# Forgetting attention and a bilinear FFN on one core: the decay moved from TensorE to a DVE pass, q and k loaded six tokens to a partition, scores and older values in one PE visit

## The chip, the cores and the metric

The kernel runs on one NeuronCore of a Trainium2 chip. The metric is device time in microseconds (us) of one execution, lower is better. The median of three runs of the kernel before is 453.05 us (452.42 to 453.66).

Engine names are those of the profile: PE is the matrix engine (PEld its weight loads), DVE the vector engine, ACT the scalar engine, POOL the GpSimd engine, and SP the engine that issues most DMAs. PSUM is the memory that matmuls write; it has eight banks of 512 float32 per partition, and all eight are in use.

## The reference

Eight batches of eight heads, 576 tokens, head dimension 64. Attention has a learned forgetting: each token has a gate f, and a score is lowered by the summed logarithms of the gates between the two tokens. Heads are joined to 512 columns per token and go through a bilinear FFN.

```python
q, k, v: (8, 8, 576, 64); f: (8, 8, 576); w_a, w_b: (512, 1536); w_out: (1536, 512)
scores = q @ k.T / sqrt(64)
cum    = cumsum(log(clip(f, 1e-4, 1)), axis=-1)
scores = where(causal, -1e9, scores + cum[..., :, None] - cum[..., None, :])
x      = softmax(scores) @ v            # heads joined: (4608, 512)
out    = ((x @ w_a) * (x @ w_b)) @ w_out
```

The row term `cum[..., :, None]` is the same for a whole row and falls out of the softmax, so that the kernel adds only the column term.

## The kernel before

**Pairs.** Two heads make a pair (four pairs in a batch, 32 in all, index t in the code). One head of a pair lies on partitions 0 to 63, the other on 64 to 127. The 576 rows of scores of a head are five blocks i of 128 (the last has 64). Causality leaves 128*(i+1) columns in block i.

**Scores (L457 to L494).** `qk_group` writes one of four groups of blocks, (1, 0), (2), (3), (4), into a PSUM tile `sc` of two banks (two such tiles). Three kinds of matmuls add up in it: q times k (`sc<-kT,qT`, and `sc<-kT,tT` for the last 64 rows, which have tiles of their own), a matrix of ones times the two float16 rows (high and low part) of the decay (`sc<-cr,ones`), and a mask of -60000 above the diagonal (`sc<-neg,low`). Each is issued twice, once for each half of the array's rows, and the two halves run side by side.

**Softmax.** `do_max` (L502) takes the negated row maximum of both heads with one DVE reduction from PSUM; `do_exp` (L527, L531) runs on ACT with the maximum as bias, reads PSUM, and sums as it goes, which makes a second instruction, ACTIVATION_READ_ACCUMULATOR; DVE takes reciprocals of the sums (L538, L540), POOL multiplies (L548). The probabilities PA and PB (float16) are transposed by DMA (L558), in batch 0 by PE (L564). `do_pv` (L588) and `do_pv4` (L601, the last 64 rows) multiply with v into one PSUM bank `pv`, and DVE copies to `xT` (L608, L612).

**FFN (L729 to L762).** `ffn(t0, n)` takes n tokens: 12 times a group of four matmuls for w_a (`psa`) and four for w_b (`psb`), an ACT copy of psa (L263), a DVE product (L743), then for each 128 tokens 12 matmuls with w_out (`pso`, L752), a copy and a store. Tokens are cut into 256, 256 and eight times 512. psa, psb, pso and the transposed tiles share three PSUM banks called `ff`.

**Inputs.** q, k, v come by DMAs from SP, 128 tokens to 128 partitions, so that a packet is the 256 bytes of one head's token. They are cast to float16 (L261 to L267; POOL from batch 1 on). q and k are transposed by PE in batches 0 and 1 (L300) and by DMA later. Weights come in 36 DMAs of 256 KB into a ring `wl` of four and are cast by DVE or POOL (L451).

**The order.** `schedule()` (L144 to L209) is a list scheduler inside the kernel. It knows a written duration for every operation, priorities, how many buffers each ring has, and the room in the DMA queue, and it places all operations in one order; each engine's queue holds its instructions in that order, and no engine overtakes. Attention has priorities by batch, and the FFN's matmuls (priority 5000 and over) fill what is left on PE. A change of PE's tile shape counts 0.1 us there.

Of the kernel before, what the change touches and what calls it, by code (L numbers as in the profile page):

```python
# [25 lines left out]
def kernel(  # L26
# [28 lines left out]
    HP = [slice(0, 64), slice(64, 128)]  # L55

# [4 lines left out]
    ones16 = perm.tile([128, 128], FP16, tag="ones16", name="ones16")  # L61
    cone = perm.tile([BH, S], FP16, tag="cone", name="cone")
# [3 lines left out]
    def constants():  # L66
        nc.gpsimd.memset(warm, 1.0)
        nc.gpsimd.memset(cone, 1.0)
        make_identity(nc, ident16)
        nc.gpsimd.memset(ones16, 0.0)  # L70
# [3 lines left out]
        for h in range(2):  # L74
            nc.gpsimd.memset(ones16[64 * h:64 * h + 2, :], 1.0)
            nc.gpsimd.affine_select(out=neg64[HP[h], :], in_=neg64[HP[h], :],
                                    compare_op=mybir.AluOpType.not_equal, fill=NEGBIG, base=0,
                                    pattern=[[-1, 64]], channel_multiplier=1)
            for half in range(2):
                x = low[half][HP[h], :]  # L80
                nc.gpsimd.affine_select(out=x, in_=x, compare_op=mybir.AluOpType.is_gt, fill=0.0,
                                        base=64 * half, pattern=[[-1, 128]], channel_multiplier=1)

    def paddings():
# [3 lines left out]
        nc.gpsimd.memset(crs[1], 0.0)  # L88
# [3 lines left out]
    wa16 = [perm.tile([128, DF], FP16, tag=f"wa16_{i}", name=f"wa16_{i}") for i in range(4)]  # L92
    wb16 = [perm.tile([128, DF], FP16, tag=f"wb16_{i}", name=f"wb16_{i}") for i in range(4)]
    wout16 = [perm.tile([128, DM], FP16, tag=f"wout16_{i}", name=f"wout16_{i}") for i in range(12)]
    nv = [perm.tile([128, NSB, H, D], FP16, tag=f"nv{i}", name=f"nv{i}") for i in range(2)]
    crs = [perm.tile([128, NP, S], FP16, tag=f"cr{i}", name=f"cr{i}") for i in range(2)]
    PB = [perm.tile([128, 13, 128], FP16, tag=f"PB{i}", name=f"PB{i}") for i in range(2)]

    RING = {"wl": 4, "n32": 4, "n16": 2, "n16t": 1, "nv": 2, "cr": 2, "qT": 2, "kT": 2, "tT": 2,
            "PA": 3, "PB": 2, "PTA": 3, "PTB": 2, "st": 6, "ht": 14, "a16": 3, "osb": 2,  # L100
            "sc": 2, "pv": 1, "ff": 3}
    wl_pool = pool("wl", RING["wl"])
    n32_pool = pool("n32", RING["n32"])
# [8 lines left out]
    dram = pool("scr", 1, space=bass.MemoryType.DRAM)  # L112
# [8 lines left out]
    PKT = {256: 0.021, 512: 0.031, 1024: 0.051, 2048: 0.095}  # L121

    class Op:


        def __init__(self, eng, dur, fn, deps=(), prio=0.0, land=None, mode=None, name="", bulk=False):
# [3 lines left out]
            self.bulk = bulk  # L130
# [12 lines left out]
    def schedule():  # L143
# [12 lines left out]
        def ready(o, e):  # L156
            t = 0.0
# [4 lines left out]
            for tag, _ in o.takes:  # L162
                lv = lives[tag]
                if len(lv) >= RING[tag]:
                    for u in lv[-RING[tag]]:
                        if u.done is None:
                            return None
                        t = max(t, u.done + SEM)
            return t

        while len(order) < len(ops):
            best = None
            for e, lst in pending.items():
                cand = None
                for o in lst:
# [3 lines left out]
                    at = max(r, free[e])  # L179
                    if o.bulk:  # L180
                        at = max(at, dma_free - BACKLOG)
                    if cand is None or at < cand[0] - 1e-9:
                        cand = (at, at + o.durs[e], o, e)
                        if at <= free[e] + 1e-9:
                            break
                if cand and (best is None or cand[0] < best[0] - 1e-9
# [6 lines left out]
            if e == "PE":  # L193
                if mode is not None and o.mode != mode:
                    at += 0.1
                mode = o.mode
            o.start = at
            free[e] = at + dur
# [18 lines left out]
    cum_d = dram.tile([2, BH, S], FP16, tag="cum_d", name="cum_d")  # L217
    cw = {}

    def f_load(_):  # L220
        for n in ("f", "l", "c"):
            cw[n] = wl_pool.tile([128, 576], FP32, tag="wl", name=f"cum_{n}")
        cw["f"], cw["l"] = cw["f"][0:BH, 0:S], cw["l"][0:BH, 0:S]
        cw["c"] = cw["c"][0:BH, :].bitcast(FP16).rearrange("p (c s) -> p c s", c=2)
        nc.sync.dma_start(out=cw["f"], in_=f.rearrange("b h s -> (b h) s"))

    def warm_table(func):
# [3 lines left out]
    o_z = Op("DVE", 1.5, lambda _: nc.vector.memset(crs[0], 0.0), prio=-300)  # L231
    o_w = Op("ACT", 1.4, warm_table(LN), [], prio=-300)
    o_f = Op("SP", 0.55, f_load, prio=-300, land=0.6)
    wl_users = [take(o_f, "wl") for _ in range(3)]
    o1 = Op("DVE", 0.45, lambda _: nc.vector.tensor_scalar(out=cw["f"], in0=cw["f"], scalar1=1e-4,
                                                           scalar2=1.0, op0=MAX, op1=MIN), [o_f], prio=-300)
    o2 = Op("ACT", 0.68, lambda _: nc.scalar.activation(out=cw["l"], in_=cw["f"], func=LN), [o1, o_w], prio=-300)
    o3 = Op("DVE", 1.35, lambda _: nc.vector.tensor_tensor_scan(
        out=cw["f"], data0=cone, data1=cw["l"], initial=0.0, op0=MUL, op1=SUB), [o2], prio=-300)
    o4 = Op("DVE", 0.45, lambda _: nc.vector.tensor_copy(out=cw["c"][:, 0, :], in_=cw["f"]), [o3], prio=-300)  # L240
    o5 = Op("DVE", 0.75, lambda _: nc.vector.tensor_tensor(out=cw["c"][:, 1, :], in0=cw["f"],
                                                           in1=cw["c"][:, 0, :], op=SUB), [o4], prio=-300)
    o6 = Op("SP", 0.55, lambda _: nc.sync.dma_start(out=cum_d.rearrange("c r s -> r c s"), in_=cw["c"]), [o5],
            land=0.6, prio=-300)
    o_e = Op("ACT", 1.4, warm_table(EXP), [o2], prio=-300)
    for u in wl_users:
        u.extend([o1, o2, o3, o4, o5, o6])
# [4 lines left out]
    cr_op, cr_users, kq_users, kq_ops, tail_op, v_ops, v_users = {}, {}, {}, {}, {}, {}, {}  # L252
    qk_ops = {}

    def n32_tile(key):
        T[key] = n32_pool.tile([128, 1024], FP32, tag="n32", name=f"{key[1]}32")
        return T[key]
# [11 lines left out]
    def load_main(b, which, sbs):  # L269
        t32 = n32_tile(("n32", which, b, sbs[0])).rearrange("p (n h d) -> p n h d", n=2, h=8)  # L270
        w = sbw[sbs[0]]
        for n, sb in enumerate(sbs):
            nc.sync.dma_start(out=t32[0:w, n],
                              in_=src_of[which][b, :, 128 * sb:128 * sb + w, :].rearrange("h s d -> s h d"))

    def cast_main(e, b, which, sbs):
        t32 = T.pop(("n32", which, b, sbs[0])).rearrange("p (n x) -> p n x", n=2)
        w, n = sbw[sbs[0]], len(sbs)
        if which == "v":
            o = nv[b % 2][0:w, sbs[0]:sbs[0] + n].rearrange("p n h d -> p n (h d)")  # L280
        else:
            if ("n16", which, b) not in T:
                T[("n16", which, b)] = n16_pool.tile([128, 4, 512], FP16, tag="n16", name=f"{which}16")
            o = T[("n16", which, b)][:, sbs[0]:sbs[0] + n]
        cast(e, o, t32[0:w, 0:n], which == "q")

    def tr_main(b, which, lo, hi):
        if ("T", which, b) not in T:
            T[("T", which, b)] = qkT_pool.tile([128, 4, NP, 128], FP16, tag=f"{which}T", name=f"{which}T")
        nc.sync.dma_start_transpose(  # L290
            out=T[("T", which, b)][:, lo:hi].rearrange("p s n c -> p (s n) c"),
            in_=T[("n16", which, b)][:, lo:hi].rearrange("p s c -> p (s c)"))

    def pe_transpose(b, which, sbs):

        p = ps.tile([128, 8, 128], FP16, tag="ff", bufs=3, name="psT")
        src = [T[("n16t", b)]] if which == "t" else [T[("n16", which, b)][:, sb] for sb in sbs]
        for m, x in enumerate(src):
            for n in range(NP):
                nc.tensor.matmul(out=p[:, NP * m + n, :], lhsT=x[:, 128 * n:128 * n + 128], rhs=ident16,  # L300
                                 is_transpose=True, start=(m + n == 0),
                                 stop=(m == len(src) - 1 and n == NP - 1), skip_group_check=True)
        T[("psT", which, b, sbs)] = p

    def pe_evict(e, b, which, sbs):
        p = T.pop(("psT", which, b, sbs))
        if which == "t":
            o = T[("tT", b)] = qkT_pool.tile([128, NP, 128], FP16, tag="tT", name="tT")
            cast(e, o, p[:, 0:NP, :], False)
            return  # L310
        if ("T", which, b) not in T:
            T[("T", which, b)] = qkT_pool.tile([128, 4, NP, 128], FP16, tag=f"{which}T", name=f"{which}T")
        cast(e, T[("T", which, b)][:, sbs[0]:sbs[-1] + 1].rearrange("p s n c -> p (s n) c"),
             p[:, 0:NP * len(sbs), :], False)

    def pe_path(b, which, sbs, deps, p):
        n = len(sbs)
        mm = Op("PE", 0.24 * n, lambda _: pe_transpose(b, which, sbs), deps + [o_c], prio=p, mode="full",
                name=f"pt{b}{which}{sbs[0]}")
        u = take(mm, "ff")  # L320
        ev = Op(None, {"DVE": 0.12 + 0.3 * n, "ACT": 0.2 + 0.4 * n}, lambda e: pe_evict(e, b, which, sbs), [mm],
                prio=p, name=f"pe{b}{which}{sbs[0]}")
        u.append(ev)
        return mm, ev

    def load_tail(b):
        t32 = n32_tile(("n32", "t", b, 0))
        for n, which in enumerate("kq"):
            nc.sync.dma_start(out=t32[64 * n:64 * n + 64, 0:512].rearrange("p (h d) -> p h d", h=8),
                              in_=src_of[which][b, :, SF:S, :].rearrange("h s d -> s h d"))  # L330

# [533 lines left out]
```

## Time and profile before

| | |
|---|---|
| median of three runs | 453.05 us (452.42 to 453.66) |
| profiled execution, its own time | 454.96 us |
| its span, first to last instruction | 453.0 us |
| busy PE, DVE, ACT, POOL | 423.6, 275.5, 252.0, 230.9 us |
| DMA packets under 512 B | 233,344 of 242,930 |
| last matmul of attention ends, last matmul of all ends | 381.7 us, 449.2 us |

The profile's page gives busy time by engine, the span in 40 slices of 11.3 us, the chain that ended last, and the costliest groups of instructions; a row of a group has the line, the engine, the operation, the tiles written and read, the shape, the count, the busy time and the mean duration in ns. The timeline gives instructions in order of time: start, duration of the merged piece, engine, line, operation, tiles, shape, count, and in brackets the idle time before it. [...]

### The profile page before, as it was taken

The numbers are of one execution on the slowest core, as the hardware profiler recorded it, in microseconds if no ns is written. First come the engines' busy times: TensorE is split into PE (matmuls) and PEld (weight loads), VectorE is DVE, ScalarE is ACT, GpSimd is POOL, SyncE is SP. The second block draws the span as 40 slices with busy tenths as digits, with TensorE's granted clock in tenths as the row PEclk, the third lists the DMA queues.
The fourth block names the chain that finished last, engine by engine and source line by source line (L and its number), as shares of the span: only waits on it lengthen the run. The fifth ranks groups of instructions, "written<-read, shape, count | busy, mean of one in ns | idle before, by whom it ended". The sixth has DMA issues, their size and how long they took to land.

```text
span 453.0 us, 10430 instructions
## 1 busy us (share of the span) xinstructions
PE 423.6 (94%) x3868; PEld 217.4 (48%) x3868; DVE 275.5 (61%) x571; ACT 252.0 (56%) x739; POOL 230.9 (51%) x395
## 2 busy tenths in 40 slices
PE   2599985699999999999999999999999999999996
PEld 1456653466444444444544444444544544444442
DVE  6589867665777576656763677667656762331331
ACT  5468966564576657637662676567646661231320
POOL 6388879563757566728553676576556540000000
PEclk9999998799999999999999999999999999999999
DMA  8999999999999999999999999899997643101002
GB/s 160 212 266 255 258 256 209 213 215 204 220 198 182 198 214 196 180 216 200 200 186 222 201 200 197 191 209 205 182 208 160 94 88 86 46 1 69 24 1 93
DMA packets 242930, 78.32 MB, mean 173 GB/s; under 512 B 233344, under 2 KB 233600, under 8 KB 242880
## 3 DMA queue, kind: packets, MB, share of 16 engines
q1 hardware_dynamic: 242880, 77.67, 85.6%
q8 instruction: 30, 0.49, 0.4%
q14 instruction: 20, 0.16, 0.1%
HBM read 38.04 MB, written 9.58 MB: 105 GB/s over the span
## 4 chain that ended last, share of the span: by engine, by line
PE 85%; DVE 5%; DMA 4%; POOL 2%; ACT 1%; issue 1%; SPq 0%; POOLq 0%; DVEq 0%
PE pso L752 21%; PE psa L732 21%; PE psb L732 21%; PE sc L463 15%; PE pv L588 4%; DMA wl<-in_moe_w_out_dram 2%; DVE st L502 2%; PE pv L601 2%; DMA k<-in_k_dram 2%; POOL PA L548 1%; PE psT L300 1%; DVE wout L451 1%; ACT PA L531 1%; PE psP L564 1%; POOL PB L548 1%
## 5 line engine op out<-in xcount | busy, mean ns | idle before, releaser
L502 DVE TENSOR_REDUCE st<-sc 128x2 f32<-128x1024 f32 (+4 forms) x160 | 125.5, 805 | 39.9 <-PE sc L463 33.3
L548 POOL TENSOR_SCALAR PA<-PA,st 128x256 f16<-128x256 f16 (+2 forms) x192 | 89.9, 482 | 85.3 <-DVE st L540 76.5
L743 DVE TENSOR_TENSOR ht<-psb,a 128x512 f16<-128x512 f32 (+1 forms) x120 | 76.3, 636 | 64.4 <-PE psb L732 59.9
L732 PE MATMUL psa<-xT,wa 128*128 128x512 f16 (+1 forms) x480 | 114.0, 360 | 0.1
L531 ACT ACTIVATE PA<-sc,st 128x256 f16<-128x256 f32 (+2 forms) x192 | 89.5, 478 | 44.1 <-DVE st L502 29.5
L732 PE MATMUL psb<-xT,wb 128*128 128x512 f16 (+1 forms) x480 | 113.5, 359 | 0.1
L263 ACT CAST a<-psa 128x512 f16<-128x512 f32 (+1 forms) x120 | 65.2, 543 | 77.9 <-PE psa L732 77.3
L752 PE MATMUL pso<-wout,ht 128*128 128x512 f16 x432 | 101.9, 380 | 3.1 <-POOL wout L451 1.7
L548 POOL TENSOR_SCALAR PB<-PB,st 128x512 f16<-128x512 f16 (+1 forms) x96 | 68.3, 723 | 27.7 <-DVE st L540 15.9
L732 PEld LDWEIGHTS <-wa 128*128 128x128 f16 x480 | 43.6, 98 | 41.2 <-issue 0.6
L732 PEld LDWEIGHTS <-wb 128*128 128x128 f16 x480 | 43.5, 98 | 41.4 <-issue 0.3
L752 PEld LDWEIGHTS <-ht 128*128 128x128 f16 x432 | 39.0, 98 | 46.6 <-issue 3.5
L531 ACT ACTIVATE PB<-sc,st 128x512 f16<-128x512 f32 x64 | 43.7, 690 | 19.6 <-issue 6.9
L463 PE MATMUL sc<-cr,ones 64*128 64x256 f16 (+5 forms) x384 | 49.2, 308 | 0.0
L463 PE MATMUL sc<-kT,qT 64*128 64x128 f16 (+3 forms) x256 | 35.6, 316 | 4.6 <-ACT PB L531 2.5
L531 ACT ACTIVATION_READ_ACCUMULATOR PA<-sc,st 128x1 f32 x192 | 39.6, 206 | 0.0
L463 PEld LDWEIGHTS <-low 64*128 64x128 f16 (+1 forms) x576 | 24.6, 101 | 16.8 <-issue 2.0
L267 DVE COPY osb<-pso 128x512 f32<-128x512 f32 x18 | 12.4, 689 | 30.6 <-PE pso L752 30.6
L463 PE MATMUL sc<-neg,low 64*128 64x64 f16 (+1 forms) x576 | 31.0, 196 | 0.0
L608 DVE CAST xT<-pv 128x512 f16<-128x512 f32 (+1 forms) x36 | 22.6, 628 | 13.6 <-PE pv L588 13.6
L263 ACT COPY osb<-pso 128x512 f32<-128x512 f32 x18 | 10.5, 586 | 36.2 <-PE pso L752 34.2
L588 PEld LDWEIGHTS <-nv 128*64 128x64 f16 x640 | 20.3, 115 | 11.1 <-issue 9.0
(77 smaller groups left out, 344.5 us busy)
## 6 DMA issues: line engine op xcount, KB each, us to landing
out_dram<-osb SPq DMA_DIRECT2D x36, 256.0 KB, 2.2
k<-in_k_dram SPq DMA_DIRECT2D x32, 256.0 KB, 4.0
q<-in_q_dram SPq DMA_DIRECT2D x32, 256.0 KB, 4.2
v<-in_v_dram SPq DMA_DIRECT2D x32, 256.0 KB, 4.0
wl<-in_moe_w_a_dram SPq DMA_DIRECT2D x12, 256.0 KB, 3.8
wl<-in_moe_w_b_dram SPq DMA_DIRECT2D x12, 256.0 KB, 3.5
wl<-in_moe_w_out_dram SPq DMA_DIRECT2D x12, 256.0 KB, 4.7
t<-in_k_dram SPq DMA_DIRECT2D x8, 128.0 KB, 3.6
```

The source lines that it names most:

```text
L263: nc.scalar.copy(out=out_, in_=in_)
L267: VEC[e].tensor_copy(out=out_, in_=in_)
L463: nc.tensor.matmul(out=dst, lhsT=lhsT, rhs=rhs, start=start, stop=stop, skip_group_check=True)
L502: nc.vector.tensor_reduce(out=m, in_=T[("s", t, i)], axis=AXX, op=MAX, negate=True)
L531: nc.scalar.activation(out=p_blocks(t, i)[:, :, h, :], in_=T[("s", t, i)][:, h, :].rearrange("p (j k) -> p j k", k=128), func=EXP, bias=st ...
L548: VEC[e].tensor_scalar(out=p, in0=p, scalar1=st[:, c:c + 1], scalar2=1.0, op0=MUL, op1=MUL)
L588: nc.tensor.matmul(out=o[HP[h], 128 * i:128 * i + 128], lhsT=vt[:, j, 2 * pr + h, :], rhs=pt[:, base_blk[i] + 2 * j + h, :], start=first, ...
L601: nc.tensor.matmul(out=o[HP[h], 0:64], lhsT=vt[:, j, 2 * pr + h, :], rhs=pb[:, 8 + j, 64 * h:64 * h + 64], start=(j == 0), stop=(j == NSB ...
L608: nc.vector.tensor_copy(out=xT[pr][:, b, c], in_=T.pop(("pv", t, rows))[:, c])
L732: nc.tensor.matmul(out=p[:, 0:n], lhsT=w16[db][:, 128 * fb:128 * fb + 128], rhs=xTflat[db][:, t0:t0 + n], start=(db == 0), stop=(db == 3))
L743: nc.vector.tensor_tensor(out=ht[:, 0:n], in0=T.pop(("psb", t0, fb))[:, 0:n], in1=T.pop(("a16", t0, fb))[:, 0:n], op=MUL)
L752: nc.tensor.matmul(out=o, lhsT=T[("ht", t0, fb)][:, 128 * tb:128 * tb + 128], rhs=wout16[fb], start=(fb == 0), stop=(fb == 11))
```

## The change

- **Decay on DVE.** `sc` holds q times k and the mask. One DVE instruction (`tensor_tensor_reduce`, L530) for each block and head reads `sc` and a float32 tile `spread` with the decay row in every partition, writes the negated sum to an SBUF tile `S` and its row minimum to `st`. ACT then takes exp(-S + minimum) from SBUF. Batch 0 keeps the decay on PE.
- **spread.** The decay is written once to DRAM in float32. For batches 2 to 7 a DMA reads one row of 1152 values into all 128 partitions (24 such DMAs, ring of three). In batch 1, PE makes it with two matmuls of 512 columns per pair (L491), and ACT or DVE copies it.
- **q and k.** A DMA loads four heads with six tokens to a partition (96 partitions, 1,536 bytes to a packet); casts are to [96, 6, 256]; PE transposes them in all batches, six 96-column transposes per pair for each of q and k, and ACT or DVE copies to `kT` and `qT`, sorting tokens as it writes (every sixth element). The tiles for the last 64 rows are gone.
- **One PE visit.** From batch 2 on, groups 0 and 1 of pair t are followed at once by pv and pv4 of pair t-2, without FFN between; pv4 goes into unused columns of the score tile. Groups 2 and 3 make the second visit.
- **Weights** come in nine DMAs of 1 MB from POOL's queue, which cast to float16 on the way; the 36 casts are gone.
- **Order.** Batch 1 is treated like batch 0, ahead of the FFN; the FFN's cuts are 256, 256, 256, 384, six times 512, 384; the scheduler prefers work of PE's present tile shape, and counts 0.04 to 0.11 us of overlap between instructions.

The core of the diff (DECP is batch 0 alone, TG is 6, W0 + WD * n is 8 + 5 n us):

```diff
-                mm(c[:, h, pos[i]], ones16[r, :], crs[b % 2][r, pr, 0:128 * (i + 1)])
+        if b in DECP:
+            for i in groups[g]:
+                for h, r in enumerate(HP):
+                    mm(c[:, h, pos[i]], pick[r, t:t + 1].to_broadcast([64, 128]), crow[r, 0:128 * (i + 1)])
...
+    def load_spread(t):
+        nc.sync.dma_start(out=spread[t % RING["bc"]], in_=cum_d[t:t + 1, :].to_broadcast([128, 2 * S]))
...
+    def do_decay(t, g, i, h):
...
+            o, x, y = T[("z", t, i)][:, h * n:h * n + n], T[("s", t, i)][:, h, :], c[:, h, 0:n]
+            m = st[:, 2 * i + h:2 * i + h + 1]
+        nc.vector.tensor_tensor_reduce(out=o, in0=x, in1=y, scale=-1.0, scalar=3e38, op0=ADD, op1=MIN, accum_out=m)
...
+            def stage(_, gs=gs, old=old):
+                for g in gs:
+                    qk_group(t, g)
+                if old is not None:
+                    do_pv(old, (0, 1, 2, 3), {"A", "B"})
+                    do_pv4(old, T.pop(("spare", t)))
...
+    def load_qk(b, which, half):
+        nc.sync.dma_start(out=x[0:96], in_=src_of[which][b, 4 * half:4 * half + 4].rearrange("h (g t) d -> g h (t d)", t=TG))
+    def pe_transpose(b, which, pr):
+        for t in range(TG):
+            nc.tensor.matmul(out=p[:, 96 * t:96 * t + 96], lhsT=x[0:96, t, 128 * (pr % 2):128 * (pr % 2) + 128],
+                             rhs=ident16[0:96, 0:96], is_transpose=True, start=(t == 0), stop=(t == TG - 1),
+                             skip_group_check=True)
+    def pe_evict(e, b, which, pr):
+        cast(e, T[("T", which, b)][:, pr, :].rearrange("p (g t) -> p t g", t=TG),
+             T.pop(("psT", which, b, pr))[:, 0:S].rearrange("p (t g) -> p t g", t=TG), False)
...
+            w_ops[key] = Op("POOL", 1.2, lambda _, src=src, dst=dst: nc.gpsimd.dma_start(out=dst, in_=src),
+                            prio=-250, land=packets(512, 2048), name=f"ldw{key[0]}{key[1]}")
+            w_ops[key].after = W0 + WD * n
```

Counts in the built programs: matmuls 3,868 before and 3,956 after; changes of tile shape between one matmul and the next 317 and 238; DVE instructions 573 and 1,029, of which 280 are the new pass and 280 its reads of the accumulated minimum, each right behind its pass.

## The prediction

> **What bounds it now.** I read the page first (engines, slices), then the stretches by window, then the timelines of PE and DVE inside a bound stretch, then the groups by shape.
>
> ```profile
> span 453.0 us, 10430 instructions
> ...
> PE 423.6 (94%) x3868; PEld 217.4 (48%) x3868; DVE 275.5 (61%) x571; ACT 252.0 (56%) x739; POOL 230.9 (51%) x395
> ...
> PE   2599985699999999999999999999999999999996
> ...
> PEclk9999998799999999999999999999999999999999
> DMA  8999999999999999999999999899997643101002
> ```
>
> PE is full from the ninth slice on; before that it has holes, and the clock row dips with them. The windows:
>
> ```profile
> 68.00:91.00 23.00, 14.48 (x178) 9.42 (x179) 16.77 (x36) 13.02 (x45) 16.96 (x28) 0.78 1.07 212
> 181.00:226.00 45.00, 45.00 (x418) 21.20 (x418) 28.96 (x61) 27.71 (x86) 26.77 (x45) 1.00 1.05 201
> 400.00:453.00 53.00, 49.16 (x228) 22.12 (x226) 14.53 (x21) 12.29 (x21) 0.00 (x0) 1.00 0.11 40
> ```
>
> From 91 us to the last matmul (449.2) PE never rests: 358 us of pure work, and 3.8 us of copy and store behind it. DVE has 29 of 45 us. In 68 to 91 PE rests 8.5 us at a granted clock of 0.78; the waits there are for `wout`, whose last cast starts at 89.5. What PE had done by 91 us, at the durations it has later, is 46 us (72 transposes of 0.057, 100 of P at 0.057, scores of seven pairs at 2.2, values of six at 1.0, 13.5 of FFN, 2 of changes). So **45 us are lost at the start** (24 of them before the first psa at 33.3), and PE's whole work is 449.2 - 45 = **404 us**.
>
> **PE's work, part by part.** A score visit in the timeline of PE:
>
> ```profile
> 250.38 1.04 PE L752 MATMUL pso<-wout,ht 128*128 128x512 f16 x4
> 251.35 0.39 PE L463 MATMUL sc<-kT,qT 64*128 64x512 f16 x2
> 251.57 0.38 PE L463 MATMUL sc<-cr,ones 64*128 64x512 f16 x2
> 251.79 0.22 PE L463 MATMUL sc<-neg,low 64*128 64x64 f16 x4
> 251.94 1.04 PE L732 MATMUL psa<-xT,wa 128*128 128x512 f16 x4
> ```
>
> Starts tell more than durations, which overlap. The decay's two matmuls take 251.79 - 251.57 = 0.22 us. Four FFN matmuls take 0.865 us where FFN follows, but 0.97 here: a change of tile shape costs 0.1 us, once going in and once coming out.
>
> - Decay matmuls gone in 28 pairs: from start to start 0.220, 0.216, 0.162, 0.110, 0.056 and 0.028 us for the six shapes, 0.79 a pair: **-22.1**.
> - Changes of shape: 317 to 238 in the built order, 79 x 0.1: **-7.9**.
> - Transposes of q and k: eight of 128 columns take 0.46 us at full clock (43.84 to 44.30), so 96 columns 0.043, six 0.26, 64 sets 16.6 us, less 72 x 0.057 now: **+12.5**.
> - Decay spread of batch 1 by PE: eight matmuls of 512 columns at 0.217: **+1.7**. The other FFN cuts add none: the columns are the same.
>
> Sum -15.8: 404 becomes 388 us. A merged visit waits on PE for the transposed P of pair t-2; behind it in PE's queue stands FFN. P's DMA lands 4.0 us after issue and has two pairs (some 24 us) of room, so I cost it at nothing; uncovered, it would be up to 4 us once per pair.
>
> **The start.** The first psa stands behind more scores than now (two pairs whole, the first rows of batch 1): some 14 us of PE's work. It needs all of q and k of batch 0, 2.4 MB against 1.0 now, in 1.5 KB packets. I take it at 40 us (bounds 33, as now, and 48): 26 us lost. After it the loss is 21 us now. In the change weights need no ring, no cast and no turn of DVE, but must pass POOL's queue, behind its products. To the end of batch 1's inputs 16.5 MB must come; at the 212 to 266 GB/s of slices 3 to 8 that is 62 to 78 us, and the large packets should do better (2 KB packets take 98 ns on one of 16 engines, 334 GB/s). PE wants `wout` at about 40 + 24 groups x 0.44 + 12 of attention = 63 us. So I keep 6 of the 21 us (bounds 0 and 21). Lost: 26 + 6 = **32 us** instead of 45.
>
> [...]
>
> **DVE, which must not become the bound.** Per pair, as occupied in its queue. Back to back, each instruction starts 0.08 us before the other's record ends:
>
> ```profile
> 234.33 0.69 DVE L743 TENSOR_TENSOR ht<-psb,a 128x512 f16<-128x512 f32 x1 [0.24 <-PE psb L732]
> 234.94 0.69 DVE L608 CAST xT<-pv 128x512 f16<-128x512 f32 x1
> 235.55 0.15 DVE L540 RECIPROCAL st<-st 128x2 f32<-128x2 f32 x1
> ```
>
> The new pass is in no row. Nearest are the sum of a PSUM and an SBUF operand, and the reduction; for its read of the minimum, DVE's smallest instruction and ACT's read:
>
> ```profile
> L743 DVE TENSOR_TENSOR ht<-psb,a 128x512 f16<-128x512 f32 x96 | 66.3, 690 | 58.8 <-PE psb L732 54.3 <-ACT a L263 3.9
> L531 ACT ACTIVATION_READ_ACCUMULATOR PA<-sc,st 128x1 f32 x192 | 39.6, 206 | 0.0
> L502 DVE TENSOR_REDUCE st<-sc 128x2 f32<-128x1024 f32 x32 | 39.0, 1220 | 10.9 <-PE sc L463 10.7
> L538 DVE RECIPROCAL st<-st 128x1 f32<-128x1 f32 x32 | 4.9, 154 | 1.3 <-ACT PB L527 1.3
> ```
>
> Reductions of 256 and 1024 take 416 and 1,220 ns: 1.05 ns an element and 0.148 fixed. Two heads of 128, 256, 384, 512 and 576 elements: 2 x (0.20 + 0.33 + 0.47 + 0.60 + 0.67) = 4.5 us after overlap, against 3.6 for today's reductions. Ten reads at 0 to 0.206; I take 0.07, the reciprocal after overlap: 0.7. With reciprocals 0.35, values 0.74, FFN for 144 tokens 2.05 + 0.34, and two thirds of two copies to kT, qT (0.37 each from the 1024-column copy's 674 ns; 0.64 if every sixth element halves the rate) 0.5 to 0.85: **9.2 us a pair** (8.5 to 10.9) against PE's 388/32 = 12.1. ACT: nine exps from SBUF cost some 0.04 more each (cast of k 617 ns against psa's 586), with the copies 7.5 us. POOL: products 4.9 and casts 2.2, 7.1 us. DMA loses some 100,000 of its 233,344 small packets for 12,288 of 1.5 KB and 3,072 of 4.6 KB. None is at 12. SP's 24 spread loads pass ahead of P's transposes in its queue; a spread waits for the passes of three pairs earlier, long done.
>
> **Sum.** 388 + 32 lost + 3.8 behind = **423 us** of span. The profiled execution took 454.96 for a span of 453.0, while the median is 453.05, the span itself; so 423 is also the time.
>
> **Rivals.**
> 1. *The start isn't shortened*: weights come no sooner, or the first psa at 48 us. Then the 45 us stay: 436. For: DMA stands at 9 tenths throughout; POOL's queue is in order. Against: the ring and 36 casts are gone.
> 2. *DVE delays PE*: reads at 0.206, slow copies, 10.9 us a pair, nine tenths of PE's step, with in-order waits; the FFN has but three `ff` banks, now shared with 48 more transposed tiles. At 1 us a pair over 24 pairs: 447. Against: the longest instruction ahead of a product falls from 1.22 to 0.75 us.
> 3. *Slower: the pass runs at two cycles an element*, in the decay step itself. 3,712 elements a pair at 1.05 ns more are 3.9 us: DVE 13.1, with a twentieth of waits 13.8 against PE's 12.1. The 1.7 us over 24 pairs are 41, the time **464**. It decides from 12.7 us of DVE a pair (with the twentieth 13.35, 1.25 a pair above PE), where the 30 us of gain are used up. Against: the product row, one operand in PSUM, one in SBUF, keeps one element a cycle.
> 4. *The start shrinks wholly* (psa at 33, `wout` never late): 408.
>
> [...]
>
> **Chances.** Forecast 0.60, rival 1 0.13, rival 2 0.12, rival 3 0.11, rival 4 0.04. Below 0.3% (what a measurement of this kernel can tell from no change) are the forecast, 1, 4 and most of 2: 0.86; same 0.03; slower 0.11. The range, 408 to 449, takes in 4, 1 and 2 and leaves out 3.
>
> **What would show it.** Score visits of PE without decay rows, six changes of shape a pair instead of ten; transposed sets of 0.26 us; PE full from about 45 us, no wait for `wout`; the pass at 0.28 to 0.75 us with a read under 0.1; DVE at three quarters in the middle windows. Wrong if PE there has holes ended by DVE, if a pass of 512 takes over 1 us, or if the first psa comes after 48 us.

## The result and the profile after

The change makes the kernel slower: **495.81 us** median (489.75 to 497.05) against 452.74 (452.37 to 453.66), a ratio of 1.092 (95% interval 1.083 to 1.101). Forecast were 423 us, faster, 408 to 449. The profiled execution took 497.05 us for a span of 495.2. Its page, from the lines that were shown of before:

```profile
span 495.2 us, 11054 instructions
...
PE 428.0 (86%) x3956; PEld 237.1 (48%) x3956; DVE 371.0 (75%) x1027; ACT 295.6 (60%) x768; POOL 229.0 (46%) x385
...
PE   1676788697979897899898979896989999999996
...
PEclk9999599889989999999989999899799999999999
```

PE is no longer full from the ninth slice on: sixes to eights stand among the nines up to the thirtieth slice (371 us), and the clock row dips there too (0.95 as the mean of 91 to 385 us, 1.00 before). Attention ends at 431.8 us, where it ended at 381.7. DVE went from 275.5 to 371 us although most of its reductions and the casts of weights are gone. The same window before and after (busy us of PE, PEld, DVE, ACT and POOL, then PE's granted clock, DMA share, GB/s):

```profile
91.00:385.00 294.00, 294.00 (x2794) 144.78 (x2793) 187.81 (x397) 177.43 (x546) 166.19 (x277) 1.00 0.99 187
91.00:385.00 294.00, 260.92 (x2575) 143.70 (x2575) 247.77 (x745) 198.62 (x525) 158.01 (x246) 0.95 0.92 195
```

From 91 to 385 us PE rests for 294 - 261 = 33 us, where it rested for nothing before. DVE has 248 of the 294 us, not 188; that is no full engine, so one looks for a long instruction and not for the sum. The groups by shape (DVE's pass, its read of the minimum, and the copies to `kT` on DVE and ACT; those to `qT` are alike):

```profile
L530 DVE CUSTOM_DVE_ANT_0 S<-sc,spread 128x512 f32<-128x512 f32 x56 | 38.3, 691 | 1.4 <-PE sc L449 1.0 <-DVE st L571 0.3
...
L308 DVE COPY kT<-psT 128x576 f16<-128x576 f16 x21 | 43.1, 2105 | 5.7 <-PE psT L341 5.5
...
L304 ACT COPY kT<-psT 128x576 f16<-128x576 f16 x11 | 22.9, 2079 | 8.1 <-PE psT L341 8.1
...
L530 DVE DVE_READ_ACCUMULATOR2_ANT st<- 128x1 f32 x224 | 18.6, 83 | 0.0
```

The pass is what the forecast said. **The copies are not: 2.1 us each on both engines**, where the forecast had 0.37 to 0.64. The 64 of them take 132 us, 88 on DVE and 44 on ACT. How 2.1 us on ACT come to stop PE is to be seen in the timeline of PE,

```profile
243.31 0.68 PE L341 MATMUL psT<-ident,k 96*128 96x96 f16 x12
243.83 1.03 PE L864 MATMUL pso<-wout,ht 128*128 128x512 f16 x4
245.91 0.42 PE L341 MATMUL psT<-ident,q 96*128 96x96 f16 x6 [1.06 <-ACT kT L304]
248.16 0.42 PE L341 MATMUL psT<-ident,q 96*128 96x96 f16 x6 [1.83 <-ACT kT L304]
```

and beside it the timeline of ACT:

```profile
243.77 2.09 ACT L304 COPY kT<-psT 128x576 f16<-128x576 f16 x1 [2.17 <-PE psT L341]
...
246.05 2.06 ACT L304 COPY kT<-psT 128x576 f16<-128x576 f16 x1
```

Two sets of k and one `pso` hold the three `ff` banks. The next set needs a bank and stands in PE's order until ACT's first copy ends (243.77 + 2.09 = 245.86; PE goes on at 245.91), the one after it until the second ends (248.11, and 248.16). Scores, which need none of these banks, stand behind, and so does FFN, which needs one. From 91 to 385 us, waits that end with a copy to `kT` or `qT`, on ACT or DVE, come to 16.2 of the 33 us. The largest single sum is another (us in total, times, longest):

```profile
PE sc L449 <- DVE st L530: 4.5, 6, 1.8
```

These are scores whose bank waits for DVE's pass; the pass has its place in DVE's order among such copies, of which two in a row take 3.98 us (from 248.52).

### The profile page after: what moved, and what is told of

Read it like the earlier page. It is cut to its first block, busy times and chain, and to the rows that moved or that the text cites. A ratio compares the mean times of both kernels' runs of the same rounds, so it can differ in the third digit from the quotient of the medians.

```text
span 495.2 us, 11054 instructions
## 1 busy us (share of the span) xinstructions
PE 428.0 (86%) x3956; PEld 237.1 (48%) x3956; DVE 371.0 (75%) x1027; ACT 295.6 (60%) x768; POOL 229.0 (46%) x385
## 5 line engine op out<-in xcount | busy, mean ns | idle before, releaser
L530 DVE CUSTOM_DVE_ANT_0 S<-sc,spread 128x256 f32<-128x256 f32 (+3 forms) x280 | 142.4, 541 | 2.4 <-PE sc L449 1.0
L844 PE MATMUL psa<-xT,wa 128*128 128x512 f16 (+2 forms) x528 | 119.9, 351 | 7.7 <-ACT kT L304 3.6
L844 PE MATMUL psb<-xT,wb 128*128 128x512 f16 (+2 forms) x528 | 120.0, 352 | 7.6 <-ACT kT L304 2.6
L304 ACT CAST a<-psa 128x512 f16<-128x512 f32 (+2 forms) x132 | 66.3, 502 | 71.7 <-PE psa L844 62.1
L855 DVE TENSOR_TENSOR ht<-psb,a 128x512 f16<-128x512 f32 (+2 forms) x132 | 78.1, 593 | 40.4 <-PE psb L844 33.7
L561 ACT ACTIVATE PA<-S,st 128x256 f16<-128x256 f32 (+2 forms) x168 | 84.6, 508 | 31.6 <-DVE st L530 27.6
L449 PE MATMUL sc<-kT,qT 64*128 64x128 f16 (+5 forms) x384 | 49.1, 315 | 13.3 <-DVE st L530 4.5
L561 ACT ACTIVATE PB<-S,st 128x512 f16<-128x512 f32 x56 | 40.5, 723 | 22.3 <-POOL PA L579 14.6
L308 DVE COPY kT<-psT 128x576 f16<-128x576 f16 x21 | 43.1, 2105 | 5.7 <-PE psT L341 5.5
L308 DVE COPY qT<-psT 128x576 f16<-128x576 f16 x22 | 44.8, 2106 | 2.3 <-PE psT L341 2.1
```

What stands on the lines that cost most here:

```text
L304: nc.scalar.copy(out=out_, in_=in_)
L308: VEC[e].tensor_copy(out=out_, in_=in_)
L449: nc.tensor.matmul(out=dst, lhsT=lhsT, rhs=rhs, start=start, stop=stop, skip_group_check=True)
L530: nc.vector.tensor_tensor_reduce(out=o, in0=x, in1=y, scale=-1.0, scalar=3e38, op0=ADD, op1=MIN, accum_out=m)
L561: nc.scalar.activation(out=p_blocks(t, i)[:, :, h, :], in_=(T[("s", t, i)][:, h, :] if direct else T[("z", t, i)][:, h * n:h * n + n]).rea ...
L844: nc.tensor.matmul(out=p[:, 0:n], lhsT=w16[:, db, 128 * fb:128 * fb + 128], rhs=xTflat[db][:, t0:t0 + n], start=(db == 0), stop=(db == 3))
```

## The experiments

All ratios are to the kernel before, run on the same chip; brackets hold the 95% interval. "PE's rest" is 294 us less its busy time from 91 to 385 us.

**Is it the copies, or the pass?** Theory A: the copies write every sixth element of float16, and that costs 2.1 us. Rival B: the pass makes DVE the bound, and the copies only show it. Four kernels: each of the two taken out alone, both together, and the sorting moved.

**e1_nosort** leaves out the sorting of tokens, so `kT` and `qT` hold the tokens in another order and the output is that of permuted scores:

```diff
-        cast(e, T[("T", which, b)][:, pr, :].rearrange("p (g t) -> p t g", t=TG),
-             T.pop(("psT", which, b, pr))[:, 0:S].rearrange("p (t g) -> p t g", t=TG), False)
+        cast(e, T[("T", which, b)][:, pr, :], T.pop(("psT", which, b, pr))[:, 0:S], False)
```

> The 64 copies from psT to kT and qT write one after the other instead of to every sixth element; the tokens of q and k then stand in another order, and this sorting is the part that is left out. Theory A (the copies' step is the cause): a copy falls from 2.1 us to about 0.45, DVE is relieved of 43 x 1.65 = 71 us and ACT of 21 x 1.6 = 34, PE's holes in the middle windows close, and the time is 425 to 440 us. Rival B (the decay pass fills DVE by itself): the copies fall but PE keeps most of its holes, 475 to 490.

Measured: 446.62 us, 0.984 (0.978 to 0.990). Its group of DVE's copies:

```profile
L308 DVE COPY kT<-psT 128x576 f16<-128x576 f16 x21 | 9.3, 452 | 12.7 <-PE psT L341 12.7
```

**e2_sortread** sorts on the reading side instead: it reads PSUM at a step of 96 elements and writes in sequence. The whole computation is there.

```diff
-        cast(e, T[("T", which, b)][:, pr, :].rearrange("p (g t) -> p t g", t=TG),
-             T.pop(("psT", which, b, pr))[:, 0:S].rearrange("p (t g) -> p t g", t=TG), False)
+        cast(e, T[("T", which, b)][:, pr, :].rearrange("p (g t) -> p g t", t=TG),
+             T.pop(("psT", which, b, pr))[:, 0:S].rearrange("p (t g) -> p g t", t=TG), False)
```

> The same copies, sorting on the reading side: PSUM is read at a step of 96 elements, kT and qT are written one element after the other; the whole computation is done. Theory A, if it is the step of the write in SBUF that costs: 0.6 to 0.7 us a copy (one element a cycle) and 430 to 445 us. If any step of this size costs, on the read as on the write: 2 us a copy and 490 to 500. Rival B: 480 to 490 with short copies.

Measured: 449.01 us, 0.991 (0.986 to 0.995): 47 us less than the change, by two index patterns, and 1% below before. The copies take 751 ns on DVE and 635 on ACT.

**e3_decpe** takes the pass away instead (decay by PE in batches 2 to 7, the change's slow copies kept), **e4_nosort_decpe** both:

```diff
-    DECP = tuple(range(1))
+    DECP = (0, 2, 3, 4, 5, 6, 7)
```

> The decay of batches 2 to 7 goes back to matmuls on PE, with the row maximum on DVE and exp from PSUM; the slow copies and all else stay. DVE gets rid of 24 x about 1.9 = 45 us, PE gets 24 x 0.79 = 19 more. Theory A: the copies still stop DVE and ACT for 2.1 us at a time, 480 to 505 us. Rival B: PE's holes close, 450 to 465.

Measured: 552.57 us, 1.215 (1.209 to 1.221).

> Both edits at once: copies without sorting (that part left out), decay of batches 2 to 7 on PE. Against the kernel with the copies alone shortened, this gives the worth of the decay pass by itself. Theory A: PE is the bound there, and 19 us more of matmuls cost 12 to 19 us: 440 to 455. Rival B: it is faster than the one with the decay pass.

Measured: 496.81 us, 1.093 (1.088 to 1.098). So A holds and B falls: shorter copies bring 49 us with the pass (495.8 to 446.6) and 56 without it (552.6 to 496.8), and taking the pass away costs 50 to 57. The signs were foreseen, the sizes were not: all four times lie above theory A's ranges, e3 and e4 by 42 to 48 us. From e1 to e4 the span grows by 44 us, of which PE's busy time takes 29.5 and its rest 15. In e4 the waits of PE name what the pass is good for beyond its matmuls: 12.1 us, from 91 to 385 us, for scores that wait for ACT's exps. Without the pass exp reads `sc` itself and holds one of its two banks until it is done.

One rival is left. The scheduler's written duration of such a copy is 0.45 us on DVE and 0.65 on ACT, which e1's copies have (452 and 635 ns) and the change's do not. So the 47 to 49 us are the price of long copies in an order laid out for short ones. No run told the scheduler 2.1 us, and what an order laid out for that would have saved is open.

**What is left between 449 and the forecast's 423?** From 91 us on, e2_sortread's window and the longest waits of its PE:

```profile
91.00:385.00 294.00, 281.59 (x2842) 153.41 (x2841) 233.85 (x814) 196.41 (x574) 168.71 (x268) 0.99 0.99 207
```

```profile
PE psT L341 <- POOL k L308: 6.0, 4, 1.7
PE psT L341 <- POOL q L306: 3.0, 4, 1.2
```

PE's rest is 12.4 us, and 9 of them are transposes whose input POOL has not cast yet, because the load came late. In the change the loads of k and q take longer to land (6.2 and 6.4 us for 576 KB) than before (4.0 and 4.2 for 256 KB); its DMA issue for k, with KB and median us to landing:

```profile
k<-in_k_dram SPq DMA_DIRECT2D x16, 576.0 KB, 6.2
```

The planner (the scheduler in the kernel) counts on 3.3 us (384 packets at 0.073 us on 16 engines, 1.75, and 1.5 more). Theory C: the rest is this order. **e5_late** is e2_sortread with 2.5 us more told to the planner, and changes nothing else:

```diff
-                o.done = dma_free + LAT
+                o.done = dma_free + LAT + (2.5 if o.name[:2] == "ld" and o.name[2] in "1234567" and o.name[3] in "qk" else 0.0)
```

> e2_sortread with one edit: the planner counts the loads of q and k of batches 1 to 7 as landing 2.5 us later (about 5.8 us after issue, against 6.4 measured in e2_sortread and about 3.3 planned there), so that it puts the six transposes and what follows them later in PE's order. Theory C (the rest of the missed forecast is PE waiting in its own order for transposes whose inputs come late from DMA, 10.3 of the 12.4 us of holes from 91 to 385 us): the holes with psT ahead of them fall below 3 us, and the time by 6 to 12 us, to 437 to 443. Rival D (DMA as a whole is late, the wait only moves to the scores or FFN behind it): the holes appear ahead of other tiles and the time stays within 446 to 452.

Measured: **437.49 us**, 0.967 (0.964 to 0.970), the fastest of all. Only 0.4 us of waits for transposes are left from 91 us on, PE's rest is 6.4 us, spread over many causes (1.2 us at most for one), and the clock row has a single dip:

```profile
34.00:44.00 10.00, 8.31 (x78) 5.56 (x78) 6.67 (x13) 6.22 (x18) 8.69 (x11) 0.50 0.99 172
...
91.00:385.00 294.00, 287.63 (x2835) 155.89 (x2834) 234.74 (x803) 192.86 (x560) 164.31 (x259) 1.00 0.97 204
```

C holds. Of the 11.7 us of span between e2_sortread and this run, 6.8 are PE's rest and 4.9 its busy time, over the whole span; the granted clock fell once more in e2_sortread, where it was 0.92 from 91 to 136 us (1.00 in e5_late). **e6_late_gate** is e5_late and frees the second halves three groups sooner (`("k", 1, 4), ("q", 1, 5)` for 7 and 8):

> e5_late with the loads of the second halves of k and q freed three groups earlier. Theory C: 0 to 3 us below e5_late, since the data is there sooner. Rival D: the same as e5_late or 1 to 4 us above it, since the earlier loads collide with the transposed P and the spreads.

Measured: 439.30 us, 0.971 (0.969 to 0.973), 1.8 above e5_late: sooner loads bring nothing more. That is what rival D gave for this run, 0 to 4 us above; the collision that D names as the reason was not looked for. For e5_late itself D is out.

**What is the merged visit worth?** **e7_nomerge** is e2_sortread, **e9_late_nomerge** e5_late, both without it:

```diff
-        if b not in EARLY and t + LAG < NP * B:
+        if False:
...
-            if gs == (0, 1) and (t - LAG) // NP not in EARLY and t >= LAG:
+            if False:
```

> e2_sortread without the merged visit: values of a pair are multiplied in a visit of their own and pv4 goes into its own bank. In the built order PE changes its tile shape 257 times instead of 206. By the forecast's 0.1 us a change: 51 more are 5 us, so 452 to 456. Rival: the merged visit binds the values to the scores and brings waits of its own, and without it the time is the same or less, 444 to 449.

Measured: 451.77 us, 1.000 (0.997 to 1.002), 2.8 above e2_sortread (4.0 by the ratios).

> e5_late without the merged visit, so the part by itself in an order in which PE no longer waits for transposes; PE changes its tile shape 254 times instead of 203. By the forecast's 0.1 us a change 5.1 us more than e5_late: 441 to 444. Rival (e7_nomerge's +2.8 us on e2_sortread was what is left of 5 after it had saved waits): up to 446. If it is at 438 or less, the merged visit is worth nothing.

Measured: 448.85 us, 0.989 (0.984 to 0.995), 11.4 above e5_late (10 by the ratios) and beyond both expectations. 51 changes of shape at 0.1 us are 5.1; PE rests 3.4 us more from 91 to 385 us, where its waits for P transposed by DMA go from 1.2 to 5.1 us; 1.5 to 3 us stay without a name.

**The start.** In e5_late the first psa comes at 47.2 us, and PE runs at a granted clock of 0.50 from 34 to 44. **e8_weights7** is e2_sortread with `W0, WD = 8, 7`, **e10_late_weights4** e5_late with `W0, WD = 6, 4`:

> e2_sortread with weights issued every 7 us from 8 us on instead of every 5. Theory S (at the start the weights take DMA from k, q and v of batches 0 and 1, so that PE waits and its clock falls): first psa 3 to 6 us sooner than at 49.6, the clock row without the half-speed stretch at 34 to 45 us, the time 2 to 6 us less unless wout is then late. Rival: PE waits for the weights instead, first psa the same or up to 2 us sooner, the time 449 to 455.

Measured: 456.76 us, 1.010 (1.006 to 1.015), above both expectations, first psa at 50.1, and the stretch of half speed only moved, to 38 to 48 us. PE's rest is 16.9 us here and 12.4 in e2_sortread: the edit changes the scheduler's order far behind the start too, so that the time does not go to the start alone.

> e5_late with weights issued from 6 us on every 4 us instead of from 8 every 5. Theory W (the slow start is PE waiting for scores' exps and first loads, and weights are there in time at 5 us a piece): within 2 us of e5_late, 436 to 440. Rival S (weights share DMA with the inputs at the start, e8_weights7 only moved that later): 440 to 446, first psa after 48 us.

Measured: 441.38 us, 0.973 (0.968 to 0.978), first psa at 48.6. S is not why the first psa is late: with fewer weights in the way it came no sooner (e8). Pulled ahead, weights put it off by 1.4 us, and the time of 441.38 lies within what S gave and 1.4 us above W's; so both a faster and a slower pace cost, and neither theory covers both. **e11_late_fill** tries the clock:

```diff
+                if b == 0:
+                    for _ in range(12):
+                        nc.tensor.matmul(out=c[:, 1, 384:512], lhsT=ident16, rhs=ident16, start=False, stop=True,
+                                         skip_group_check=True)
```

> e5_late with 12 further matmuls of 128 columns, whose results nobody reads, behind each of the 12 score visits of batch 0: 0.65 us a visit at full clock, 8 us in all, most of it in time in which PE waits for exps. Theory H (the clock falls to half at 34 to 45 us because PE rested too much in the microseconds before, 1.6 of 4 us busy): the stretch of half speed is gone or shorter by over half, first psa at 44 to 47 instead of 47.2, the time 432 to 438. Rival (the fall has another cause, or the added work costs more than the clock gives): the stretch stays, 439 to 445.

Measured: 444.99 us, 0.979 (0.972 to 0.987), the rival's time, first psa at 51.7. The fall at 34 us is gone, but now the clock is at 0.50 from 20 to 26 us and near it (0.57) from 40 to 44: some ten microseconds as before. In e5_late PE was busy 1.6 of the 4 us ahead of the fall; in e11_late_fill 1.8 of 4 ahead of the first (from 16 to 20 us) and 2.3 of 4 ahead of the second. How idle PE has to be for the clock to fall is not shown: e5_late is as idle from 16 to 20 us (1.6 of 4), and its granted clock is 1.00 there. What decides between two equally idle stretches is open.

**What does a step in the writing cost?** **e13_steps** is e5_late with copies of 192 elements behind everything else:

```diff
+                for st in (1, 2, 3, 4, 6, 8):
+                    cast(e, w16[:, 0:192 * st].rearrange("p (n s) -> p n s", s=st)[:, :, 0], p[:, 0:192], False)
+            for st in (2, 4, 6):
+                cast(e, w32[:, 0:192 * st].rearrange("p (n s) -> p n s", s=st)[:, :, 0], p[:, 0:192], False)
```

> e5_late with copies added behind everything else: 192 elements of a transposed tile in PSUM written to SBUF as float16 at steps of 1, 2, 3, 4, 6 and 8 elements (twice) and as float32 at steps of 2, 4 and 6, on DVE and on ACT; the float16 ones also on POOL from float32 in SBUF; and on DVE float16 in groups of two and of three neighbours, a group every six. What counts is the duration of each copy. From the change's copies (2.1 us for 576 at step 6, 0.45 in sequence on DVE) step 6 should take some 0.7 us and step 1 some 0.2. [...] Rival P (the price grows with the distance): steps 2, 3 and 4 in between, about in proportion. [...]

The same copies in an earlier form, e12_steps, gave no result. DVE's timeline, instruction by instruction (float16 at steps 1 and 6; float32 at step 6; float16 in groups of two, a group every six):

```profile
438.20 0.26 DVE L308 COPY PB<-psX 128x192 f16<-128x192 f16 x1
...
440.03 0.80 DVE L308 COPY PB<-psX 128x192 f16<-128x192 f16 x1
...
442.61 0.49 DVE L308 CAST spread<-psX 128x192 f32<-128x192 f16 x1
...
454.96 0.28 DVE L308 COPY PB<-psX 128x192 f16<-128x192 f16 x1 [11.85 <-POOL PB L308]
```

| step, elements | 1 | 2 | 3 | 4 | 6 | 8 |
|---|---|---|---|---|---|---|
| DVE, float16, ns | 258 | 372 | 479 | 583 | 796 | 1,006 |
| ACT, float16, ns | 318 | 373 | 478 | 583 | 795 | 1,007 |
| POOL, float16 from float32 in SBUF, ns | 342 | 398 | 502 | 609 | 822 | 1,032 |
| DVE, float32, ns | - | 556 | - | 494 | 494 | - |

Rival P holds for float16: from step 2 on, each element of distance costs 104 to 107 ns for 192 elements, some 0.55 ns an element, on all three engines alike. Steps 2 to 4 lie in between, as P has it (372, 479 and 583 ns on DVE, against 258 in sequence and 796 at step 6). P did not foresee the rest: float32 shows no such rise from 8 to 24 bytes of distance (556, 494 and 494 ns), and float16 in neighbouring pairs takes 285 ns where single elements take 796 (in threes 372).

## Why the prediction was wrong, step by step

- **The step that failed** is in the sum for DVE and ACT: "copies to kT, qT (0.37 each from the 1024-column copy's 674 ns; 0.64 if every sixth element halves the rate)". They take 2.1 us. The size in sequence was right: e1's copies have 0.45 us, 0.37 after an overlap of 0.08. What failed is the upper bound, which came from the thought that a step costs at most a halved rate; no row of before wrote with a step, and that should have led to a wider bound. With copies of 0.45 to 0.75 us the same program takes 446.6 to 449.0, 47 to 49 of the 73 us between 423 and 495.8.
- The harm is not the 88 us of DVE. With 2.1 us a copy the forecast's own sum gives DVE 9.2 - 0.5 + 2.7 = 11.4 us a pair, still under PE's 12.1 and under the 12.7 from which rival 3 would cost all of the gain. PE waits in its order for single blocks of 2.1 us, also on ACT, whose sum has room. Rival 2 had the mechanism (in-order waits, three `ff` banks shared with the transposes) but priced it with 0.64 us copies, at 24 us. The forecast took comfort from DVE's longest instruction ahead of a product falling from 1.22 to 0.75 us; it rose to 2.1 instead. The waits cost twice: PE's 3,956 matmuls are busy for 428.0 us in the change and 409.7 in e2_sortread, so that of 47 us of span 29 are rest and 18 slower matmuls. By the mean granted clocks (0.959 and 0.977) an estimated 8 of the 18 are the clock's; the other 10 have no name.
- "It needs all of q and k of batch 0" was seen for the start, but behind it the new transposes were costed as PE work only. **They also put a load and a POOL cast ahead of PE's queue**, where the kernel before transposed by DMA, off PE's path, in six of eight batches. That is the second term that was left out: 11.5 us, e2_sortread to e5_late (10.6 by the ratios).
- **The first psa**: forecast 40 (33 to 48), measured 59.5, with short copies 49.6, and 47.2 in e5_late. Even without the copies it lies at the upper bound. In e5_late PE waits 8.5 us for the first k, 4.9 us for exps that hold batch 0's score banks, and runs ten microseconds at half speed. The first is no new cost (10.5 us in two waits before); the other two were not priced.
- No wait for `wout`: right, in the change with luck. None is among PE's waits from 45 to 91 us; its first pso comes 25 us behind the first psa (59.5, 84.4), where the forecast had 23 (40, 63). But the last load of `wout` is issued at 66.3 us, too late for 63; in e5_late it is issued at 52.9 and would have been in time. The forecast's reading of before was right in part only: of some 8 us of PE's waits from 68 to 91 us, 2.9 end with casts of `wout` and 4.7 with exps that hold score banks, which sooner weights do not shorten.
- Of PE's parts, the decay, the transposes and the visit came out as forecast. The visit in the timeline of PE:

```profile
230.80 0.34 PE L449 MATMUL sc<-kT,qT 64*128 64x256 f16 x4
230.97 0.28 PE L449 MATMUL sc<-neg,low 64*128 64x64 f16 x8
...
231.40 0.36 PE L619 MATMUL pv<-PTA,nv 128*64 128x128 f16 x6
...
232.24 3.63 PE L864 MATMUL pso<-wout,ht 128*128 128x512 f16 x16
```

  No decay rows, scores and older values without FFN between; and two sets of transposes start 0.52 us before what follows (243.31 to 243.83), 0.26 each as forecast. The merged visit gives more than its changes of shape, 10 to 11 us in e5_late's order. The 388 us as a whole were not measured by themselves.
- **The pass** (rival 3): right. 286 ns for 128 elements, 691 for 512, 751 for 576, so 1.05 ns an element; the read of the minimum has 83 ns, but the next pass starts with it (233.27 both), so it costs the queue nothing, against 0.07 forecast. Rival 3's two cycles an element are shown by no run, and DVE's own clock is in no trace: the "cycle" that the prediction counts with is the 1.05 ns an element of the reductions before, and the pass, with one source in PSUM and one in SBUF, kept that rate.
- DVE per pair: 371.0/32 = 11.6 us by its records against 9.2 (8.5 to 10.9); with e2_sortread's copies 10.0. POOL 229/32 = 7.2 against 7.1: right. ACT 9.2 against 7.5; with e2_sortread's copies 8.4, still 0.9 above.
- "None is at 12", of DMA: as a rate true, but the larger loads land 6.3 us after issue instead of 4, and that is what counts for a step that waits for one.

What stays of the 15.0 us between the profiled execution of e5_late (437.96) and the forecast: 6.4 us are PE's rest from 91 to 385 us, 1.7 lie outside its span, and the rest, some 7, is put down to the start, with the half-speed stretch in it. That last part is a balance, which takes the forecast's 388 us for granted, and was not tested by itself.

## What to carry to other kernels

Before a copy is made to sort, look at which side has the step: a copy of 576 float16 took DVE 0.45 us in sequence, 0.75 with the step in reading PSUM and 2.1 with the step in writing, and sorting on the reading side took two index patterns and gave 47 us. Price what an engine in order waits for by the longest single block behind which its ring can be, not by the sum of the other engine's work. When a step moves onto the bounding engine, its input's way (load, cast) comes along: order it by the landing time that the trace shows.

## What the runs showed of the hardware

- In e13_steps, copies of 192 single float16 elements to SBUF took longer the wider the step: from step 2 to step 8 some 0.55 ns an element for each element of distance, on DVE, ACT and POOL alike (DVE: 258 ns in sequence, 372 at step 2, 1,006 at step 8). Pairs of neighbours cost nearly nothing (285 against 258 ns). Float32 on DVE showed no such rise (556 ns at 8 bytes of step, 494 at 16 and at 24).
- Reading PSUM at a step of 96 float16 elements took DVE 751 ns for 576 (e2_sortread), against 451 in sequence (e1_nosort), and ACT 635 in both runs.
- The granted clock was 0.50 for about ten microseconds in e5_late, behind 4 us in which PE was busy for 1.6; behind another 4 us with 1.6 busy it stayed at 1.00. Work put into the start (e11_late_fill) did not shorten the time at half speed, but moved it: 0.50 from 20 to 26 us and 0.57 from 40 to 44, instead of 0.50 from 34 to 44.
